# Folding the attention matrix into w_in: fp32 products, and three passes over two rounded parts

## The chip, the cores and the metric

The kernel runs on one core of a Trainium2 chip. The metric is the device time of one execution in microseconds. A core has TensorE (PE in the profile; its weight loads are PEld), VectorE (DVE), ScalarE (ACT), GpSimd (POOL) and the queue SP, from which all large transfers of this kernel are started.

## What is computed

The reference, cut to what matters (all operands are drawn at random; N = 6016 tokens, C = 256):

```python
qn = q / (norm(q, axis=1) + 1e-6);  kn = k / (norm(k, axis=1) + 1e-6)
a = softmax(kn.T @ qn / tau)             # 256 x 256
x = v @ a                                # 6016 x 256
h = x @ w_in                             # w_in 256 x 2048
x = maximum(0.01 * h, h) @ w_out         # w_out 2048 x 256
g = 1 / (1 + exp(-(x @ w_gate)))         # w_gate, w_val 256 x 1536
out = (g * (x @ w_val)) @ w_out2         # w_out2 1536 x 256
```

`w_in` and the other feed-forward weights come as 64-bit floats.

## The kernel before, in words

**Attention.** In the first 40 us the 6016 rows of q and k stream in, TensorE sums their products in fp32, and VectorE their squares. A short chain then makes `e`, the exponentials of the 256 x 256 scores, in two halves of 128 rows, and `zs`, the reciprocals of the row sums. TensorE turns each half (L398), and ScalarE copies it to `eT[i]` (L401).

**W'.** v @ a is never formed. Instead the kernel multiplies a into w_in once: W' = a @ w_in, 256 x 2048, in eight column groups j of 256. `w_half(j, i, o)` (L217) makes half i of W' of group j: two fp32 products (L221) of `eT[i]` with the columns of `win[j]`, 128x256 each; `w_prime` makes both halves side by side in PSUM bank b. The groups 0 and 1 are made in the preparation, in banks y0 to y3; the other six one by one in the loop over vT pair 0, group j + 2 in the turn of group j. `w_evac` (L258) takes W' out of PSUM on ScalarE, scaled by `zs`, and `split_blocks` (L241, L242) rounds it.

**Two rounded parts.** From W' on, all large products are made of two parts of each operand: `high` is a rounding to float32r on ScalarE, `low` the remainder, a subtraction on VectorE or GpSimd. Three matmuls (low x high, high x low, high x high) make one product; see `Core.mul` (L472), `Plain.block` (L523) and `Group.sum` (L573 to L576).

**Units.** A `Unit` is one 256 x 512 or 512 x 256 piece of a 64-bit weight. `act` (L170, L172) reads its two halves of each word on ScalarE; `join` (L176, L177, L183) puts them together as fp32 on VectorE, in a tile `s`. `win[j]` is the joined tile of unit `ins[j]`, and TensorE reads it as it is. A joined unit of w_out1 (`outs1`) is split into `wo` by a cast on VectorE (L206) and a subtraction on GpSimd (L207).

**Stages.** The tokens are worked through in six pairs of 512 + 512 (the last 448 + 448), first the two layers of the first network (kind 1), then the gated one (kind 2). In kind 1 a turn is one pair and one group j of 256 columns. In pair 0 a turn has four plain blocks (`Plain`: banks d, b, then a, c), six matmuls each; in later pairs and in kind 2 a seven-product scheme (`Core`).

**What sets the order.** The schedule is written by hand: each engine carries out its instructions in the order of the code. A turn j of pair 0 (L709 to L753) is, on TensorE: blocks d and b; the sums of the keys 22 and 12 of the turn before (L573 to L576); W' of group j + 2 in bank b; the sums of the keys 11 and 21; blocks a and c (in turn 0 there are no sums, and a and c come ahead of W'). ScalarE: `g22`, `g12` out of d and b (L554), their high parts `gh` (L548), the `act` of two units, `w_evac`, the split of W', then `g11`, `g21` and theirs. VectorE: the low parts `gl` of 22 and 12 (L549), the joins of two units and the cast of a `wo`, the low part of the split of W', `gl` of 11 and 21, and the low part of the block sums (L273). GpSimd: the subtraction of `wo` (L207) and the block sums (L264 to L267). The two units of turn j are `ins[j + 3]` and `outs1[j + 1]`. A bank is given on only when its reader is done: W' of group j + 2 needs `g12` read out of b, and block b of the next turn needs `w_evac`.

**End of the preparation** (L407 to L436). On VectorE: the join of `outs1[0]` (L424), the splits of W' of groups 0 and 1, the low parts of the tokens B11 and B21, the join of `ins[2]`. Pools: `s` has three buffers; the tile `w8` of 4 KB per partition (one buffer) is used only in later pairs.

Of the kernel before, what the change touches and what calls it, by code (L numbers as in the profile page):

```python
# [12 lines left out]
F32 = mybir.dt.float32  # L13
F32R = mybir.dt.float32r
I32 = mybir.dt.int32
U32 = mybir.dt.uint32
AF = mybir.ActivationFunctionType
ALU = mybir.AluOpType
# [4 lines left out]
P = 128  # L23
N = 6016
C = 256
F1 = 2048
F2 = 1536
KC = C // P
CH = 512
# [28 lines left out]
def attention_two_ffn(ctx, tc, q, k, vT, tau, w_in, w_out1, w_gate, w_val, w_out2, outT):  # L58
# [19 lines left out]
    nc = tc.nc  # L78

    def f32(ap):  # L80
        return ap.bitcast(F32)
# [7 lines left out]
    ps = ctx.enter_context(tc.tile_pool(name="ps", bufs=1, space=PSUM))  # L89
    cctx = ctx.enter_context(ExitStack())  # L90
    cv = cctx.enter_context(tc.tile_pool(name="cv", bufs=2, side=right))
    eT = [cv.tile([P, C], F32, name=f"eT{i}", bufs=1) for i in range(KC)]

    tau_sb = const.tile([P, 1], F32, name="tau_sb")
    zs = [const.tile([P, 1], F32, name=f"z{i}") for i in range(KC)]
# [50 lines left out]
    def cols(w, j):  # L146
        return w.bitcast(I32)[:, j * 512:(j + 1) * 512].rearrange("(a p) f -> p a f", p=P)

    def rows(w, j):
        return w.bitcast(I32)[j * 256:(j + 1) * 256, :].rearrange("(a p) f -> p a f", p=P)  # L150

    class Unit:
# [19 lines left out]
            nc.scalar.activation(self.c, lo.bitcast(U32), AF.Copy, scale=2.0**-29)  # L172

        def begin_join(self):
            s = self.s = cv.tile([P, CH], I32, tag="s", name="s", bufs=3)
            nc.vector.tensor_scalar(s, self.hi, -0x80000000, None, ALU.bitwise_and)  # L176
            nc.vector.scalar_tensor_tensor(  # L177
                s, self.x.bitcast(I32), 3, s, ALU.logical_shift_left, ALU.bitwise_or
            )
# [35 lines left out]
    win = {}  # L215

    def w_half(j, i, o):  # L217

        w = f32(win[j]).rearrange("p (a b) -> p a b", a=2)
        for jj in range(KC):  # L220
            nc.tensor.matmul(  # L221
                o, eT[i][:, jj * P:(jj + 1) * P], w[:, jj, :], start=jj == 0, stop=jj == KC - 1
            )
        return o

    def w_prime(j, wp):
        return [w_half(j, i, wp[:, i * 256:(i + 1) * 256]) for i in range(KC)]

    ins = [Unit(cols(w_in, j)) for j in range(G1)]
    outs1 = [Unit(rows(w_out1, j)) for j in range(G1)]  # L230
# [13 lines left out]
    def split_half(j, i, wp):  # L244

        src = wp.rearrange("p (a b) -> p a b", a=2)
        st, a = s1_t[j], a21_t[j]
        todo = [(st[:, :, 1:3], src)]
        if i == 0:
            todo = [(a[:, :, 0:1], src[:, 0:1]), (st[:, :, 0:1], src[:, 1:2])]  # L250
        for o, x in todo:
            nc.scalar.activation(o[:, 0], x, AF.Copy, scale=zs[i])
        for o, x in todo:
            nc.vector.scalar_tensor_tensor(o[:, 1], x, zs[i], f32(o[:, 0]), ALU.mult, ALU.subtract)
# [24 lines left out]
    with tc.manual_schedule():  # L279


        with ExitStack() as actx:
# [3 lines left out]
            sm = actx.enter_context(tc.tile_pool(name="sm", bufs=1))  # L286
# [36 lines left out]
            for gi, g in enumerate(GROUPS):  # L323
# [5 lines left out]
                for nm, src in (("k", kt), ("q", qt)):  # L329
                    a = accs[nm]  # L330
                    s2 = sq.tile([P, 4, C], F32, tag="s2" + nm, name="s2")
                    nc.scalar.activation(s2[:, :g, :], src[:, :g, :], AF.Square)
                    w = min(g, WIDTH[gi])
# [3 lines left out]
                    if gi + 1 < ng and WIDTH[gi + 1] < WIDTH[gi]:  # L337
                        w = WIDTH[gi + 1]
# [16 lines left out]
            for j, (nm, i) in enumerate((("k", 0), ("k", 1), ("q", 0), ("q", 1))):  # L355
                s = slice(i * P, (i + 1) * P)
# [18 lines left out]
            )  # L375
            rq = sm.tile([P, C], F32, name="rq")
            e_sb = []

            def scaled(i):
                s_sb = sm.tile([P, C], F32, tag=f"s_sb{i}", name="s_sb")  # L380
# [40 lines left out]
            turned(1)  # L421
            for w in (B12, B22):
                tok.low(w, nc.vector)
            o1_0 = outs1[0].join()  # L424
            split_half(0, 0, wp0[0][0])
            inverse(1)
            for j in range(2):
# [5 lines left out]
            split_half(1, 1, wp0[1][1])  # L433
            for w in (B11, B21):
                tok.low(w, nc.vector)
            win[2] = ins[2].join()  # L436


        s_b = ctx.enter_context(tc.tile_pool(name="s_b", bufs=5, reuse_waits="tile"))
# [5 lines left out]
        def o_tile(name):  # L445
            return op.tile([P, 2, 2, C], F32R, tag="o", name=name)
# [217 lines left out]
        for i, (kind, p, j) in enumerate(groups):  # L664
# [44 lines left out]
            if kind == 1 and p == 0:  # L709
# [21 lines left out]
                unsummed = unsummed[len(now):]  # L731
                for w, jj, u in units:
                    if w == "in":
                        win[jj] = u.join()
                    else:
                        o1_t[jj] = o_tile("wo")
                        split_rows(u.join(), o1_t[jj], nc.gpsimd)
# [142 lines left out]
```

## Time and profile before

| | us |
|---|---|
| median of 3 runs | 1094.44 (1094.23 to 1094.81) |
| the profiled execution | 1093.51 |
| its span, first to last instruction | 1091.4 |
| TensorE busy | 1081.2 (99%) |
| VectorE busy | 774.6 (71%) |
| ScalarE busy | 604.6 (55%) |
| GpSimd busy | 522.2 (48%) |
| DMA, share of 16 engines (the kernel's main queue) | 21.6% |

The profiled execution is one run of its own, 0.93 us below the median. The granted TensorE clock is 1.00 of full speed in every stretch of it. A busy share is an average over stages with different limits; the rows further down are taken from the stretch that the change touches. Start times are microseconds from the first instruction. Matmul records overlap: the time from one start to the next is what one costs in a row of them.

### The profile page before, as it was taken

Reading aid. Unit: us, or ns where it says so; the run is one execution under the profiler, and the core shown is the slowest. Engines: PE = TensorE matmul, PEld = TensorE weight load, DVE = VectorE, ACT = ScalarE, POOL = GpSimd, SP = SyncE. Lnnn points to the kernel's source line nnn. Section 1 sums busy time; section 2 is a strip of 40 time slices with the busy share of each in tenths; the row PEclk is TensorE's granted clock in tenths of the full one; section 3 lists DMA queues with packets and bytes.
Section 4 is the critical chain, followed back from the end, with each engine's and each line's share of the span. In section 5 each row is a group of like instructions: output and inputs, shape, how many; then the busy total and the mean of one; then the engine's idle time right before and its main releaser. Section 6 shows DMA issues by size and latency. Waiting matters only on the chain.

```text
span 1091.4 us, 13956 instructions
## 1 busy us (share of the span) xinstructions
PE 1081.2 (99%) x4842; PEld 907.2 (83%) x4842; DVE 774.6 (71%) x1059; ACT 604.6 (55%) x1055; POOL 522.2 (48%) x435
## 2 busy tenths in 40 slices
PE   9999999999999999999999999999999999999998
PEld 8878888888878888879988888888888888888997
DVE  7899945785776766773467777687677677667765
ACT  7787655676665675665553444454354345344433
POOL 0155327567657658656544424433534532443333
PEclk9999999999999999999999999999999999999999
DMA  9632221224241224238430001002002001000100
GB/s 351 256 113 81 78 77 53 92 58 145 89 153 49 78 73 145 73 112 322 155 135 1 1 20 59 1 0 77 1 1 77 1 1 47 27 1 1 39 1 35
DMA packets 31495, 84.01 MB, mean 77 GB/s; under 512 B 3008, under 2 KB 5824, under 8 KB 31424
## 3 DMA queue, kind: packets, MB, share of 16 engines
q1 hardware_dynamic: 31392, 83.11, 21.6%
q8 instruction: 38, 0.62, 0.2%
q14 instruction: 33, 0.27, 0.1%
q0 software_dynamic: 32, 0.00, 0.0%
HBM read 56.62 MB, written 26.48 MB: 76 GB/s over the span
## 4 chain that ended last, share of the span: by engine, by line
PE 92%; DVE 4%; DMA 2%; ACT 1%; issue 1%; SPq 0%; ACTq 0%; DVEq 0%
PE c L472 13%; PE y L576 13%; PE d L472 13%; PE y L573 13%; PE y L574 13%; PE a L472 13%; PE b L472 7%; DMA kt<-in_k 2%; PE wp L221 1%; PE a L523 1%; PE c L523 1%; PE b L523 1%; PE d L523 1%; DVE accq L336 1%; PE s L315 1%
## 5 line engine op out<-in xcount | busy, mean ns | idle before, releaser
L573 PE MATMUL y<-gh,wo 128*128 128x512 f32 (+1 forms) x672 | 259.8, 387 | 0.0
L574 PE MATMUL y<-gh,wo 128*128 128x512 f32 (+1 forms) x672 | 258.8, 385 | 0.0
L549 POOL TENSOR_TENSOR gl<-v,gh 128x512 fp32r<-128x512 f32 (+1 forms) x76 | 107.2, 1410 | 292.1 <-issue 187.1
L576 PE MATMUL y<-gl,wo 128*128 128x512 f32 (+1 forms) x672 | 205.2, 387 | 0.0
L472 PE MATMUL c<-tok,s 128*128 128x512 f32 (+1 forms) x672 | 186.3, 385 | 3.0 <-DVE c L501 2.9
L472 PE MATMUL d<-tok,s 128*128 128x512 f32 (+1 forms) x672 | 186.2, 385 | 0.0
L472 PE MATMUL a<-tok,s 128*128 128x512 f32 (+1 forms) x672 | 185.9, 385 | 0.0
L501 DVE TENSOR_TENSOR c<-u,c 128x512 f32<-128x512 f32 (+1 forms) x112 | 75.6, 675 | 138.9 <-PE c L472 133.5
L472 PEld LDWEIGHTS c<-tok,s 128*128 128x128 f32 x672 | 125.8, 188 | 27.6 <-DVE c L501 4.2
L576 PEld LDWEIGHTS y<-gl,wo 128*128 128x128 f32 x672 | 125.4, 188 | 25.9 <-POOL gl L549 2.8
L472 PEld LDWEIGHTS d<-tok,s 128*128 128x128 f32 x672 | 125.9, 188 | 24.0 <-DVE u L506 0.8
L573 PEld LDWEIGHTS y<-gh,wo 128*128 128x128 f32 x672 | 126.2, 188 | 23.5
L574 PEld LDWEIGHTS y<-gh,wo 128*128 128x128 f32 x672 | 126.2, 188 | 23.4
L472 PEld LDWEIGHTS a<-tok,s 128*128 128x128 f32 x672 | 126.2, 188 | 23.4
L549 POOL TENSOR_TENSOR gl<-c,gh 128x512 fp32r<-128x512 f32 (+1 forms) x76 | 99.9, 1314 | 83.3 <-ACT gh L548 50.0
L486 DVE TENSOR_TENSOR u<-u,a 128x512 f32<-128x512 f32 (+1 forms) x112 | 75.2, 671 | 38.8 <-PE a L472 35.7
L549 POOL TENSOR_TENSOR gl<-u,gh 128x512 fp32r<-128x512 f32 (+1 forms) x75 | 97.5, 1300 | 0.0
L472 PE MATMUL b<-tok,s 128*128 128x512 f32 (+1 forms) x336 | 92.9, 385 | 0.0
L483 ACT COPY u<-b 128x512 f32<-128x512 f32 (+1 forms) x112 | 64.8, 579 | 48.2 <-PE b L472 48.0
L548 ACT CAST gh<-v 128x512 fp32r<-128x512 f32 (+1 forms) x76 | 46.5, 612 | 78.3 <-DVE v L832 75.5
L489 DVE TENSOR_TENSOR v<-u,c 128x512 f32<-128x512 f32 (+1 forms) x112 | 75.7, 676 | 13.6 <-DVE u L486 0.5
L491 DVE TENSOR_TENSOR v<-v,d 128x512 f32<-128x512 f32 (+1 forms) x112 | 75.7, 676 | 11.7
(125 smaller groups left out, 1522.1 us busy)
## 6 DMA issues: line engine op xcount, KB each, us to landing
wr<-in_moe_w_out SPq DMA_DIRECT2D x14, 512.0 KB, 4.1
g_d<-st SPq DMA_DIRECT2D x6, 896.0 KB, 3.6
v_d<-st SPq DMA_DIRECT2D x6, 896.0 KB, 3.6
s<-g_d SPq DMA_DIRECT2D x6, 896.0 KB, 5.6
s<-v_d SPq DMA_DIRECT2D x6, 896.0 KB, 6.3
x_d<-o SPq DMA_DIRECT2D x20, 256.0 KB, 3.2
outT<-o SPq DMA_DIRECT2D x20, 256.0 KB, 2.0
kt<-in_k SPq DMA_DIRECT2D x9, 512.0 KB, 9.8
```

What stands on the lines that cost most here:

```text
L472: nc.tensor.matmul(o[:, :n], self.st[:, w, kind, :], t[:, x, :n], start=first and i == 0, stop=i == 2, skip_group_check=not first,)
L483: nc.scalar.copy(u[:, :n], self.b[:, :n])
L486: nc.vector.tensor_tensor(u[:, :n], u[:, :n], self.a[:, :n], ALU.add)
L489: nc.vector.tensor_tensor(v[:, :n], u[:, :n], self.c[:, :n], ALU.add)
L491: nc.vector.tensor_tensor(v[:, :n], v[:, :n], self.d[:, :n], ALU.add)
L501: nc.vector.tensor_tensor(t[:, :n], self.u[:, :n], self.c[:, :n], ALU.add)
L523: nc.tensor.matmul(o[:, :self.n], w, x, start=i == 0, stop=i == len(todo) - 1)
L548: nc.scalar.copy(gh[:, :n], src[:, :n])
L549: eng.tensor_tensor(gl[:, :n], src[:, :n], f32(gh[:, :n]), ALU.subtract)
L573: nc.tensor.matmul(acc[c, m][:, :n], wo[:, 1, e, s[m]], gh, start=first, stop=False)
L574: nc.tensor.matmul(acc[c, m][:, :n], wo[:, 0, e, s[m]], gh, start=False, stop=False)
L576: nc.tensor.matmul(acc[c, m][:, :n], wo[:, 0, e, s[m]], gl, start=False, stop=stop)
```

## The change

The six products of W' from group 2 on are made of rounded parts, like the others. `eT[i]` gets a split copy `eTr[i]` (high on ScalarE, low on VectorE) at the end of the preparation. Each `win[j]`, j from 2, goes through `split_win`: the high part is a cast on ScalarE, the low part a subtraction on GpSimd, into the one buffer of tag `w8`. `w_half` then issues six float32r matmuls in three passes where it issued two fp32 ones. `eT` moves to the pool `sm`, which closes with the attention part; `s` has two buffers instead of three. The join of `outs1[0]` moves from ahead of the splits of W' to behind the join of `ins[2]`.

```diff
--- before.py
+++ after.py
@@ -89,7 +89,8 @@
     ps = ctx.enter_context(tc.tile_pool(name="ps", bufs=1, space=PSUM))
     cctx = ctx.enter_context(ExitStack())
     cv = cctx.enter_context(tc.tile_pool(name="cv", bufs=2, side=right))
-    eT = [cv.tile([P, C], F32, name=f"eT{i}", bufs=1) for i in range(KC)]
+    eT = []
+    eTr = [cv.tile([P, 2, C], F32R, name=f"eTr{i}", bufs=1) for i in range(KC)]
 
     tau_sb = const.tile([P, 1], F32, name="tau_sb")
     zs = [const.tile([P, 1], F32, name=f"z{i}") for i in range(KC)]
@@ -172,7 +173,7 @@
             nc.scalar.activation(self.c, lo.bitcast(U32), AF.Copy, scale=2.0**-29)
 
         def begin_join(self):
-            s = self.s = cv.tile([P, CH], I32, tag="s", name="s", bufs=3)
+            s = self.s = cv.tile([P, CH], I32, tag="s", name="s")
             nc.vector.tensor_scalar(s, self.hi, -0x80000000, None, ALU.bitwise_and)
             nc.vector.scalar_tensor_tensor(
                 s, self.x.bitcast(I32), 3, s, ALU.logical_shift_left, ALU.bitwise_or
@@ -216,11 +217,22 @@
 
     def w_half(j, i, o):
 
-        w = f32(win[j]).rearrange("p (a b) -> p a b", a=2)
-        for jj in range(KC):
-            nc.tensor.matmul(
-                o, eT[i][:, jj * P:(jj + 1) * P], w[:, jj, :], start=jj == 0, stop=jj == KC - 1
-            )
+        if j < 2:
+            todo = [(eT[i], f32(win[j]))]
+        else:
+            todo = [(eTr[i][:, x], win[j][:, w]) for x, w in ((1, 0), (0, 1), (0, 0))]
+        todo = [
+            (a[:, jj * P:(jj + 1) * P], b[:, jj * 256:(jj + 1) * 256])
+            for a, b in todo for jj in range(KC)
+        ]
+        for t, (a, b) in enumerate(todo):
+            nc.tensor.matmul(o, a, b, start=t == 0, stop=t == len(todo) - 1)
+        return o
+
+    def split_win(s):
+        o = cv.tile([P, 2, CH], F32R, tag="w8", name="win", bufs=1)
+        nc.scalar.copy(o[:, 0], f32(s))
+        nc.gpsimd.tensor_tensor(o[:, 1], f32(s), f32(o[:, 0]), ALU.subtract)
         return o
 
     def w_prime(j, wp):
@@ -375,6 +387,7 @@
             )
             rq = sm.tile([P, C], F32, name="rq")
             e_sb = []
+            eT += [sm.tile([P, C], F32, name=f"eT{i}") for i in range(KC)]
 
             def scaled(i):
                 s_sb = sm.tile([P, C], F32, tag=f"s_sb{i}", name="s_sb")
@@ -421,7 +434,6 @@
             turned(1)
             for w in (B12, B22):
                 tok.low(w, nc.vector)
-            o1_0 = outs1[0].join()
             split_half(0, 0, wp0[0][0])
             inverse(1)
             for j in range(2):
@@ -433,7 +445,11 @@
             split_half(1, 1, wp0[1][1])
             for w in (B11, B21):
                 tok.low(w, nc.vector)
-            win[2] = ins[2].join()
+            for a, b in zip(eT, eTr):
+                nc.scalar.copy(b[:, 0], a)
+                nc.vector.tensor_tensor(b[:, 1], a, f32(b[:, 0]), ALU.subtract)
+            win[2] = split_win(ins[2].join())
+            o1_0 = outs1[0].join()
 
 
         s_b = ctx.enter_context(tc.tile_pool(name="s_b", bufs=5, reuse_waits="tile"))
@@ -731,7 +747,7 @@
                 unsummed = unsummed[len(now):]
                 for w, jj, u in units:
                     if w == "in":
-                        win[jj] = u.join()
+                        win[jj] = split_win(u.join())
                     else:
                         o1_t[jj] = o_tile("wo")
                         split_rows(u.join(), o1_t[jj], nc.gpsimd)
```

What stands where on VectorE at the end of the preparation and at the start of turn 0, before (`wr_384` is `outs1[0]`, `wr_386` is `ins[2]`, `wr_559` and `wr_568` are `ins[3]`, `s_485` is the joined `outs1[0]`; its join stands 11 rows further up, ahead of the splits of W'):

```order
L143 TENSOR_TENSOR tok_503<-raw_380,tok_503 128x512
L143 TENSOR_TENSOR tok_505<-raw_380,tok_505 128x512
L176 TENSOR_SCALAR s_515<-wr_386 128x512
L177 SCALAR_TENSOR_TENSOR s_515<-x_475,s_515 128x512
L183 ISA s_515<-s_515,c_477 128x1024
L206 CAST wo_538<-s_485 128x512
L549 TENSOR_TENSOR gl_601<-g22_596,gh_600 128x512
L549 TENSOR_TENSOR gl_605<-g12_598,gh_604 128x512
L176 TENSOR_SCALAR s_631<-wr_559 128x512
```

and with the change:

```order
L450 TENSOR_TENSOR eTr0_75<-eT0_424,eTr0_75 128x256
L450 TENSOR_TENSOR eTr1_76<-eT1_425,eTr1_76 128x256
L177 TENSOR_SCALAR s_517<-wr_386 128x512
L178 SCALAR_TENSOR_TENSOR s_517<-x_477,s_517 128x512
L184 ISA s_517<-s_517,c_479 128x1024
L177 TENSOR_SCALAR s_524<-wr_384 128x512
L178 SCALAR_TENSOR_TENSOR s_524<-x_440,s_524 128x512
L184 ISA s_524<-s_524,c_442 128x1024
L207 CAST wo_547<-s_524 128x512
L565 TENSOR_TENSOR gl_618<-g22_613,gh_617 128x512
L565 TENSOR_TENSOR gl_622<-g12_615,gh_621 128x512
L177 TENSOR_SCALAR s_648<-wr_568 128x512
```

Two subtractions for eTr and the join of `outs1[0]` now stand between the tokens' low parts and `gl` of turn 0, and the join of `ins[3]` is behind them.

ScalarE at the same place, before (`d_563` and `b_570` are the blocks of turn 0, `x_608` belongs to `ins[3]`):

```order
L252 ACTIVATE s_467<-wp_498,z1_79 128x256 [waits PE_49]
L554 ACTIVATE g22_596<-d_563 128x512 [waits PE_49,Activation_49]
L554 ACTIVATE g12_598<-b_570 128x512 [waits PE_49,Activation_49]
L548 CAST gh_600<-g22_596 128x512 [waits Activation_49]
L548 CAST gh_604<-g12_598 128x512 [waits Activation_49]
L170 ACTIVATE x_608<-wr_559 128x512 [waits DMAHW7_49]
```

and with the change:

```order
L264 ACTIVATE s_469<-wp_496,z1_79 128x256 [waits PE_49]
L449 CAST eTr0_75<-eT0_424 128x256 [waits Activation_49]
L449 CAST eTr1_76<-eT1_425 128x256 [waits Activation_49]
L234 CAST win_521<-s_517 128x512 [waits DVE_49]
L570 ACTIVATE g22_613<-d_572 128x512 [waits DVE_49,PE_49]
L570 ACTIVATE g12_615<-b_579 128x512 [waits PE_49]
L564 CAST gh_617<-g22_613 128x512 [waits Activation_49]
L564 CAST gh_621<-g12_615 128x512 [waits Activation_49]
L171 ACTIVATE x_625<-wr_568 128x512 [waits DMAHW7_49]
```

`g22` and `g12` of turn 0 stand behind the cast of win[2], which waits for VectorE's join of `ins[2]`.

ScalarE further on in turn 0, before (`wp_591` and `wp_600` are W' of group 2 in bank b):

```order
L258 ACTIVATE wt_620<-wp_459,z0_78 128x256
L258 ACTIVATE wt_620<-wp_495,z1_79 128x256
L258 ACTIVATE wt_623<-wp_460,z0_78 128x256
L258 ACTIVATE wt_623<-wp_498,z1_79 128x256
L258 ACTIVATE wt_642<-wp_591,z0_78 128x256 [waits PE_49]
L258 ACTIVATE wt_642<-wp_591,z1_79 128x256
L241 CAST a21_646<-wt_642 128x128 [waits Activation_49]
L241 CAST s_645<-wt_642 128x384 [waits Activation_49]
L554 ACTIVATE g11_651<-a_577 128x512
```

and with the change:

```order
L270 ACTIVATE wt_637<-wp_461,z0_78 128x256
L270 ACTIVATE wt_637<-wp_493,z1_79 128x256
L270 ACTIVATE wt_640<-wp_462,z0_78 128x256
L270 ACTIVATE wt_640<-wp_496,z1_79 128x256
L234 CAST win_652<-s_648 128x512 [waits DVE_49,PE_49,Pool_49]
L270 ACTIVATE wt_662<-wp_600,z0_78 128x256
L270 ACTIVATE wt_662<-wp_600,z1_79 128x256
L253 CAST a21_666<-wt_662 128x128 [waits Activation_49]
L253 CAST s_665<-wt_662 128x384 [waits Activation_49]
L570 ACTIVATE g11_671<-a_586 128x512
```

The cast of win[3], with waits for VectorE, TensorE and GpSimd, stands ahead of the two instructions that empty bank b. The later turns have the same form.

## Rows read from the trace of the kernel before

**Rows 1.** Busy line of the page: busy us (share of the span) xinstructions, by engine.

```profile
PE 1081.2 (99%) x4842; PEld 907.2 (83%) x4842; DVE 774.6 (71%) x1059; ACT 604.6 (55%) x1055; POOL 522.2 (48%) x435
```

**Rows 2.** Table by stretch, vT pair 0: busy us (instructions) of each engine.

```profile
core 0: us, PE busy (x) PEld busy (x) DVE busy (x) ACT busy (x) POOL busy (x), PEclk, DMA share, GB/s
...
67.40:80.20 12.80, 12.77 (x57) 10.64 (x57) 12.28 (x16) 9.83 (x21) 9.59 (x12) 1.00 0.40 134
```

**Rows 3.** Waits of 57 to 133 us: who waited for whom, us, times, longest.

```profile
ACT a L241 <- PE c L523: 16.5, 5, 4.0
...
PEld wp L221 <- ACT g L554: 0.5, 1, 0.5
PEld b L523 <- ACT wt L258: 0.4, 1, 0.4
```

**Rows 4.** Chain that ended last, 0 to 180 us: start, us, what.

```profile
59.97 1.73 PE wp L221 x8
...
63.07 1.66 PE b L523 x6
...
67.48 1.99 PE wp L221 x8
```

**Rows 5.** The same chain, three matmuls of 512 and of 448 columns.

```profile
148.56 0.68 PE c L472 x3
...
1041.33 0.61 PE d L472 x3
```

**Rows 6.** Timeline of VectorE, 56 to 65 us: start, us, line, out<-in, xcount.

```profile
56.44 1.28 DVE L143 TENSOR_TENSOR tok<-raw,tok 128x512 fp32r<-128x512 f32 x2
57.64 0.42 DVE L176 TENSOR_SCALAR s<-wr 128x512 int32<-128x512 int32 x1
...
59.44 0.42 DVE L206 CAST wo<-s 128x512 fp32r<-128x512 f32 x1
59.78 2.36 DVE L549 TENSOR_TENSOR gl<-g,gh 128x512 fp32r<-128x512 f32 x2
62.06 0.69 DVE L176 TENSOR_SCALAR s<-wr 128x512 int32<-128x512 int32 x1
...
64.41 0.68 DVE L176 TENSOR_SCALAR s<-wr 128x512 int32<-128x512 int32 x1
```

**Rows 7.** Timeline of ScalarE, 53 to 68 us: also [idle before <-releaser].

```profile
53.46 0.48 ACT L252 ACTIVATE s<-wp,z 128x256 fp32r<-128x256 f32 x1 [1.01 <-DVE z L405]
...
60.75 2.27 ACT L258 ACTIVATE wt<-wp,z 128x256 f32<-128x256 f32 x6
62.89 0.32 ACT L241 CAST a<-wt 128x128 fp32r<-128x128 f32 x1
...
66.84 0.59 ACT L554 ACTIVATE g<-b 128x512 f32<-128x512 f32 x1
67.32 1.13 ACT L548 CAST gh<-g 128x512 fp32r<-128x512 f32 x2
```

**Rows 8.** Timeline of GpSimd, its subtraction of 128x512, twice.

```profile
59.99 1.60 POOL L207 TENSOR_TENSOR wo<-s,wo 128x512 fp32r<-128x512 f32 x1 [19.86 <-DVE wo L206]
...
123.38 1.40 POOL L207 TENSOR_TENSOR wo<-s,wo 128x512 fp32r<-128x512 f32 x1 [4.86 <-DVE wo L206]
```

**Rows 9.** Timeline of VectorE, 120 to 132 us, and one row of TensorE.

```profile
120.80 0.42 DVE L176 TENSOR_SCALAR s<-wr 128x512 int32<-128x512 int32 x1
...
122.88 0.43 DVE L206 CAST wo<-s 128x512 fp32r<-128x512 f32 x1
123.22 0.42 DVE L176 TENSOR_SCALAR s<-wr 128x512 int32<-128x512 int32 x1
...
126.20 0.43 DVE L206 CAST wo<-s 128x512 fp32r<-128x512 f32 x1
...
130.07 1.82 DVE L549 TENSOR_TENSOR gl<-g,gh 128x512 fp32r<-128x512 f32 x2
...
131.62 0.62 PE L576 MATMUL y<-gl,wo 128*128 128x512 f32 x2
```

## The prediction

> **What bounds the kernel now.** I read first the page's busy line: TensorE is busy 1081.2 of 1091.4 us [rows 1]. So a microsecond of TensorE work taken out, or of waiting put in, moves the end by a microsecond unless it sits in the first 57 us, where TensorE still waits for data. All the products that change lie between 59 and 120 us, so I read that stretch next. The table by stretch shows that there VectorE is as full as TensorE: 12.28 of 12.80 us [rows 2]. The list of waits of 57 to 133 us says whether that busy time hides slack: none of its six rows is VectorE's, so it runs one instruction after the other for all that time; TensorE waits for ScalarE twice, 0.5 and 0.4 us; ScalarE alone has room, 16.5 us in five waits for TensorE [rows 3]. So three engines run a tight relay in vT pair 0: TensorE fills bank b, ScalarE empties it, VectorE makes the low parts that TensorE needs one turn later. The chain shows the handovers: W' of group 2 at 59.97, then block b of the next turn at 63.07, W' of group 3 at 67.48 [rows 4]. Both later ones use bank b, and both waited for ScalarE [rows 3].
>
> **TensorE's part.** One of six products today is 8 records in 1.73 us, 0.216 each (each fp32 product is two passes) [rows 4]. The change issues 12 one-pass matmuls of 256 columns. No row has that form. Three float32r matmuls of 512 columns take 0.68, of 448 columns 0.61 [rows 5]: 0.227 and 0.203 each, so 64 columns are worth 0.024 and 256 columns come to 0.13. That is 1.56 per product, 0.17 less, 1.0 us over six. Lower bound 0.11, half of the 512-column row; upper bound 0.216, what one fp32 pass over 256 columns takes today. I take 0.13, because both float32r rows are of the very instruction, with other weights before each, and only the column count differs.
>
> **The preparation.** The join of the first w_out1 unit leaves its place ahead of the first split of W'. ScalarE waited 1.01 us for VectorE's reciprocal there [rows 7]; what then limits is the W' product itself, so the rest comes some 0.25 us earlier (an estimate; it lies between 0 and 0.3). The last `low` on VectorE then ends at 57.4 instead of 57.64 [rows 6].
>
> From there I follow one chain, in the order of the listing ahead of this:
>
> - Two eT subtractions, 128x256. The nearest row is 1.28 for two of 128x512 [rows 6], so 0.3 each, with overhead up to 0.42; 0.35 gives 58.1.
> - Join of ins[2]: 57.64 to 59.44, 1.80 [rows 6]: 59.9.
> - ScalarE's new cast of 128x512 waits for it: 0.6, as the gh casts (1.13 for two) [rows 7]: 60.5. Behind it on ScalarE stand g22 and g12 of turn 0, which used to start at once. They take 0.49 and 0.59 [rows 7], so bank b, which W' of group 2 needs, is free at 61.6, not before 59.97. GpSimd's remainder (1.40 and 1.60 on the nearest rows, for the same shape [rows 8]) ends near 62; W' of group 2 ends near 63.5 instead of 61.70.
> - VectorE: the moved w_out1 join, 1.80 alone. GpSimd's new subtraction falls on it. What that costs is shown by two joins of one turn (5): 120.80 to 122.88, 2.08, with GpSimd idle (4.86 us ahead of 123.38 [rows 8]); 123.22 to 126.20, 2.98, under GpSimd's subtraction of 1.40 [rows 8, 9]. So 0.9 more: 62.6. Then the cast, 0.34: 62.95; gl22 and gl12 as before, 2.28: 65.2; join of ins[3] as before, 2.35: 67.6, where it ends at 64.41 before [rows 6]. VectorE is now 3.2 late.
> - ScalarE's cast for win[3] waits for that join: 68.2. The evacuation of W' of group 2 stands *behind* it: two instructions, 0.38 each (2.27 for six [rows 7]): 69.0. Block b of turn 1 needs the bank: 69.0 instead of 63.07. **TensorE is 5.9 us late.**
> - W' of group 3 waits for g12 of turn 1, which follows that evacuation by 4.5 us (62.89 to 66.84 plus 0.59 [rows 7]): 73.5 instead of 67.48, 6.0 late. The five products that are left give back 5 x 0.17: **5.1 late** by this chain.
>
> **A second chain, VectorE.** It has no wait until after 133 us, so nothing absorbs what is added: 3.2 late after turn 0, and five more subtractions on GpSimd, each issued while VectorE joins the w_out1 unit, at 0.9: 7.7 late. The low part of key 11 of turn 5 was ready at about 131.0 (130.07 and half of 1.82 [rows 9]), and TensorE's use of it starts at 131.62 [rows 9]: 0.6 of slack. So this chain puts TensorE 7.1 late. The two chains overlap and do not add; the later one counts. After 133 us VectorE has its waits back, TensorE is dense to the end, and what was lost stays lost.
>
> **Hidden, costed at nothing:** the eT casts on ScalarE (they end before the VectorE work that they feed), the five later casts of win on ScalarE themselves (0.6 each, beside its 16.5 us of waits [rows 3]; without that cover 3 us), the pair of `s` buffers in place of three (the readers on GpSimd are done a join earlier), the later loads of the units (they are issued later with the joins, and need not land until some 4 us after).
>
> **Sum.** +7.1 us. On the profiled execution, 1093.51, that is 1100.6; the median of the runs shown is 0.93 above it, 1094.44 + 7.1 = **1101.5 us**. Bounds: if a GpSimd subtraction costs VectorE nothing, the second chain has 2.3 - 0.6 = 1.7 and the first decides, with 5.0 at block b and 4.2 at the end: 1098.6. If it costs its whole 1.40, 2.3 + 6 x 1.40 - 0.6 = 10.1: 1104.5. With 0.216 a matmul the first chain decides, as rival 3 works out: 1104.7.
>
> The row says that 0.9 of GpSimd's 1.40 us are lost. [...]
>
> **Rivals.**
>
> 1. *The cover holds; not slower.* TensorE's gain of 1.0 and the 0.25 of the preparation come through: 1093.2, within 0.2%. The point that decides is ScalarE's cast ahead of the evacuation: the join of ins[3] must end by 61.7, so that 0.6 and 0.75 more still meet 63.07. For it: the work is only moved or given to engines with idle time. Against it: I get 67.6, and even before the change that join ended at 64.41 [rows 6]. Chance 0.05.
> 2. *VectorE's fullness is elastic.* Its instructions stretch beside GpSimd, and re-timed they might run at their short durations (gl pair 1.28, join 2.08). Then only the moved and the waiting work stays: joins to 59.9 and 61.7, cast 62.05, gl 63.3, join 65.4, ScalarE's cast and evacuation 66.8: 3.7 late, 3.8 at W' of group 3, 3.0 at the end: 1097.4. Against it: GpSimd gets more work there, not less. Chance 0.09.
> 3. *The passes are not cheaper.* If a float32r matmul of 256 columns took what one fp32 pass takes, 0.216, a product would be 2.59, 0.86 more: 6.0 + 5 x 0.86 = 10.3, 1104.7. This is also the case of the change not doing what it says. Against it: float32r at 512 columns is one record of 0.227 [rows 5]. Chance 0.06.
> 4. *Whole exclusion*: each GpSimd subtraction stops VectorE for all of its 1.40 us: 1104.5, as above. For it: VectorE's pair took 2.36 under one of 1.60 and 1.28 without [rows 6, 8], so 1.08 were lost; against it: the join's 0.9. Chance 0.08. [...]
>
> **How the numbers follow.** The forecast, both chains at work, has 0.72. The range from 1097.0 to 1104.7 takes in the bounds of lock and matmul, and leaves out rival 1, half of rival 2 and what lies above 3 and 4. A measurement of this kernel tells about 0.2%, 2.2 us, from no change: up to 1096.6 is "same". Forecast, rivals 3 and 4 and most of rival 2 are slower: 0.90; rival 1 and the rest of 2 are the same: 0.08; faster would need more than TensorE has to gain: 0.02.
>
> **What would show it.** In the changed profile: ScalarE's first win cast starting near 59.9 and g22 only behind it; a TensorE gap of several us ahead of block b of turn 1, ended by ScalarE's `wt`; W' as 12 records at about 0.13; joins of the w_out1 units near 3.0 instead of 2.0; VectorE still without a wait near 130 and later than before by more than TensorE's 0.6 of slack. I am wrong if block b of turn 1 starts within 2 us of 63.07, if TensorE shows no wait longer than 1 us after 60 us, or if VectorE's lateness does not grow from turn to turn.

## The result and the profile after

| | before | after |
|---|---|---|
| median, same chip (6 runs each) | 1094.38 us (1093.54 to 1094.81) | 1102.11 us (1100.86 to 1103.87) |
| ratio after / before, 95% interval | | 1.0072 [1.0062, 1.0082] |
| profiled execution; its span | 1093.51; 1091.4 | 1100.86; 1098.9 |

The change makes the kernel slower by 7.7 us, 0.7%. Forecast were 1101.5 us, 7.1 more than before, in a range of 1097.0 to 1104.7. Of the six runs of the changed kernel, three lie at 1100.9 to 1101.3 with a mean granted clock of 0.997 and three at 1102.9 to 1103.9 with 0.995; the profile is one of the first three.

The page of the changed kernel: the busy line (as [rows 1]), and the chain that ended last, by engine.

```profile
PE 1083.6 (99%) x4866; PEld 908.5 (83%) x4866; DVE 780.6 (71%) x1061; ACT 608.3 (55%) x1063; POOL 530.1 (48%) x441
...
PE 85%; DVE 9%; DMA 2%; ACT 2%; issue 2%; SPq 0%; DVEq 0%; ACTq 0%
```

The chain of the kernel before:

```profile
PE 92%; DVE 4%; DMA 2%; ACT 1%; issue 1%; SPq 0%; ACTq 0%; DVEq 0%
```

TensorE is "99% busy" before and after; that line shows nothing. The chain does: VectorE's share of it was 4% before and is 9% now. Followed in order of time, the path that sets the end runs on VectorE from 56 to 118 us, over ScalarE's casts and evacuations to 130, and on VectorE again to 138.6.

The list of waits of 57 to 150 us, the longer ones of TensorE and ScalarE (who waited for whom, us in total, times, longest):

```profile
ACT win L234 <- DVE s L184: 17.7, 6, 4.3
...
PE b L539 <- ACT wt L270: 3.0, 2, 2.6
...
PE wp L229 <- ACT g L570: 1.9, 1, 1.9
```

TensorE waited 0.5 us at most in this stretch [rows 3]. Now it has two gaps, of 1.9 and 2.6 us, and both are the relay over bank b (a third wait for the bank, 0.4, comes at 120). The same list for VectorE is empty from 57 to 143 us.

TensorE's timeline, the rows that answer to [rows 4]:

```profile
61.63 3.06 PE L229 MATMUL wp<-win,eTr 128*128 128x256 f32 x12 [1.87 <-ACT g L570]
64.49 1.31 PE L539 MATMUL d<-tok,a 128*128 128x512 f32 x3
...
69.10 2.93 PE L539 MATMUL b<-tok,s 128*128 128x512 f32 x6 [2.62 <-ACT wt L270]
71.83 0.60 PE L589 MATMUL y<-gh,wo 128*128 128x512 f32 x1
...
140.57 1.53 PE L539 MATMUL a<-tok,s 128*128 128x512 f32 x6
```

The last of them is block a of turn 6, the first block behind all products of W'. In the kernel before it stood here:

```profile
133.44 1.52 PE L523 MATMUL a<-tok,s 128*128 128x512 f32 x6
```

Block b of turn 1 starts 6.0 later than at 63.07. And it takes 2.93 in place of 1.66, W' of group 2 3.06. Why, the table by stretch shows (busy us of each engine, then PEclk, the granted clock):

```profile
59.90:61.60 1.70, 0.00 (x0) 0.00 (x0) 1.63 (x4) 1.62 (x4) 0.93 (x1) 1.00 0.00 0
61.60:64.50 2.90, 2.81 (x13) 2.60 (x14) 2.87 (x4) 2.90 (x6) 1.75 (x2) 0.57 0.00 0
...
66.50:69.10 2.60, 0.00 (x0) 0.00 (x0) 2.30 (x4) 1.41 (x4) 2.52 (x4) 0.95 0.70 201
69.10:71.90 2.80, 2.80 (x7) 2.23 (x8) 2.69 (x4) 2.74 (x7) 1.71 (x2) 0.50 0.63 188
```

TensorE does nothing in the first and the third row, and behind each gap its granted clock falls, to 0.57 in the second row and to 0.50 in the fourth; before, it was 1.00 throughout.

VectorE's timeline at the same place, and GpSimd's:

```profile
52.26 0.35 DVE L266 SCALAR_TENSOR_TENSOR a<-wp,z,a 128x128 fp32r<-128x128 f32 x1 [1.69 <-ACT s L264]
...
57.40 0.75 DVE L450 TENSOR_TENSOR eTr<-eT,eTr 128x256 fp32r<-128x256 f32 x2
58.07 0.42 DVE L177 TENSOR_SCALAR s<-wr 128x512 int32<-128x512 int32 x1
...
61.04 1.65 DVE L184 CUSTOM_DVE_ANT_0 s<-s,c 128x1024 uint16<-128x1024 uint16 x1
62.72 0.43 DVE L207 CAST wo<-s 128x512 fp32r<-128x512 f32 x1
63.06 2.38 DVE L565 TENSOR_TENSOR gl<-g,gh 128x512 fp32r<-128x512 f32 x2
65.37 0.41 DVE L177 TENSOR_SCALAR s<-wr 128x512 int32<-128x512 int32 x1
...
69.18 1.55 DVE L184 CUSTOM_DVE_ANT_0 s<-s,c 128x1024 uint16<-128x1024 uint16 x1
...
137.59 1.81 DVE L565 TENSOR_TENSOR gl<-g,gh 128x512 fp32r<-128x512 f32 x2
```

```profile
60.67 1.47 POOL L235 TENSOR_TENSOR win<-s,win 128x512 fp32r<-128x512 f32 x1 [20.76 <-ACT win L234]
63.28 1.61 POOL L208 TENSOR_TENSOR wo<-s,wo 128x512 fp32r<-128x512 f32 x1 [1.15 <-DVE wo L207]
...
68.45 1.72 POOL L235 TENSOR_TENSOR win<-s,win 128x512 fp32r<-128x512 f32 x1
```

The last step of a w_out1 join (L184) takes 0.69 alone and 1.55 to 1.65 under GpSimd's new subtraction, in all six turns. Lay the three pairs of rows side by side: GpSimd ends at 62.14, 64.89 and 70.17, and the VectorE instruction that was issued meanwhile at 62.69, 65.44 and 70.73, each time 0.55 behind it. At the end of pair 0 VectorE makes the first low part of key 11 of turn 5 at 137.59 in place of 130.07 [rows 9]: 7.52 late.

ScalarE's timeline, the two casts and what stands behind them:

```profile
59.98 0.62 ACT L234 CAST win<-s 128x512 fp32r<-128x512 f32 x1 [3.76 <-DVE s L184]
60.50 0.59 ACT L570 ACTIVATE g<-d 128x512 f32<-128x512 f32 x1
60.99 0.59 ACT L570 ACTIVATE g<-b 128x512 f32<-128x512 f32 x1
...
67.69 0.62 ACT L234 CAST win<-s 128x512 fp32r<-128x512 f32 x1 [1.33 <-DVE s L184]
68.22 0.83 ACT L270 ACTIVATE wt<-wp,z 128x256 f32<-128x256 f32 x2
```

ScalarE stood idle for 3.8 us with g22 and g12 behind the cast, and later for 1.3 with the evacuation of bank b behind the next.

From there TensorE's lateness goes: W' of group 3 at 74.79 (7.3 late), of group 5 at 99.47 (6.6), of group 6 at 111.81 (6.3), block a of turn 6 at 140.57 in place of 133.44 (7.1). Between groups 4 and 6 it regains 0.28 a turn. At turn 5 it loses 0.5 at block b, which waits for an evacuation behind a win cast, which waits for VectorE's join; 0.3 at W' of group 7; and 0.4 at key 11, where it waits for VectorE's first low part. After turn 6 the instructions of both kernels run at the same distance, but for one wait of 0.3 at 487 us, to the end: 7.5.

### The profile page after: what moved, and what is told of

It is laid out like the page before. It is cut to its first block, busy times and chain, and to the rows that moved or that the text cites. A ratio compares the mean times of both kernels' runs of the same rounds, so it can differ in the third digit from the quotient of the medians.

```text
span 1098.9 us, 14010 instructions
## 1 busy us (share of the span) xinstructions
PE 1083.6 (99%) x4866; PEld 908.5 (83%) x4866; DVE 780.6 (71%) x1061; ACT 608.3 (55%) x1063; POOL 530.1 (48%) x441
## 4 chain that ended last, share of the span: by engine, by line
PE 85%; DVE 9%; DMA 2%; ACT 2%; issue 2%; SPq 0%; DVEq 0%; ACTq 0%
PE d L488 13%; PE c L488 13%; PE a L488 13%; PE y L592 12%; PE y L589 12%; PE y L590 12%; PE b L488 7%; DMA qt<-in_q 2%; DVE gl L565 2%; DVE s L184 1%; DVE s L178 1%; DVE s L177 1%; DVE tok L144 1%; DVE s L254 1%; PE s L327 1%
```

## The experiments

All kernels are edits of the changed one. "Late" is against the profile of before. Profiles differ by up to 0.6 us in when the preparation ends (the low parts of the last tokens start at 56.20 in the profile of after, 56.15 to 56.83 in the others), and why is not shown; so a few tenths of any single start mean nothing.

| kernel | median us | ratio to before | block b of turn 1: start, its record | key 11 of turn 5, VectorE | block a of turn 6 |
|---|---|---|---|---|---|
| before | | | 63.07, 1.66 | 130.07 | 133.44 |
| after | 1102.11 | 1.0072 | 69.10, 2.93 | 137.59 | 140.57 |
| cast late | 1102.69 | 1.0078 [1.0063, 1.0093] | 67.03, 2.92 | 138.46 | 141.39 |
| remainder on VectorE | 1100.65 | 1.0061 [1.0044, 1.0077] | 68.88, 1.66 | 136.27 | 139.22 |
| no remainder | 1098.98 | 1.0043 [1.0028, 1.0058] | 68.81, 1.67 | 133.44 | 137.73 |
| no moved join | 1101.18 | 1.0062 [1.0047, 1.0077] | 68.27, 2.93 | 137.14 | 140.11 |
| gaps filled | 1101.66 | 1.0065 [1.0049, 1.0080] | 69.55, 1.66 | 138.08 | 141.03 |

The median of before was 1093.6 beside the four in the middle, 1094.75 beside the last.

### The win cast behind the evacuation

```diff
-                        win[jj] = split_win(u.join())
+                        held = (jj, u.join())
...
                     w_evac(wt, wp)
+                    if held is not None:
+                        win[held[0]] = split_win(held[1])
```

> In the turns of vT pair 0 the cast of win (and with it GpSimd's subtraction) stands behind the evacuation of W' on ScalarE instead of ahead of it. Two chains: block b of turn 1 starts near 67.2 instead of 69.10 and no longer at half clock, and yet the end hardly moves, since VectorE is as late as before (first gl of key 11 of turn 5 at 137.6, within 0.5) and TensorE must wait for it there, now longer: block a of turn 6 at 140.6 again, 1101.5 to 1102.5 us. Relay alone (only the cast ahead of the evacuation costs): 1.9 from the bank and 1.4 from the clock come back, 1098.8 us.

The relay was relieved as meant: block b of turn 1 came 2.1 sooner, W' of group 5 at 97.75 (4.9 late in place of 6.6). The end did not follow: TensorE stood still again, for ScalarE's g12, for GpSimd's remainder and longest for VectorE's low part, in TensorE's timeline:

```profile
123.84 0.50 PE L229 MATMUL wp<-win,eTr 128*128 128x256 f32 x2 [0.71 <-ACT g L570]
124.64 1.45 PE L229 MATMUL wp<-win,eTr 128*128 128x256 f32 x10 [0.29 <-POOL win L235]
...
139.45 0.73 PE L592 MATMUL y<-gl,wo 128*128 128x512 f32 x2 [1.55 <-DVE gl L565]
```

So the relay alone does not set the time; VectorE's chain does. Two things came otherwise than expected: block b's record was as long as at the clock of 0.50 in the changed kernel (2.92, and 2.93 there), and VectorE was 0.87 later than after, where at most 0.5 was allowed. Why it lost more is not worked out here.

### The remainder of win on VectorE

```diff
-        nc.gpsimd.tensor_tensor(o[:, 1], f32(s), f32(o[:, 0]), ALU.subtract)
+    def low_win(o, s):
+        nc.vector.tensor_tensor(o[:, 1], f32(s), f32(o[:, 0]), ALU.subtract)
```

(called behind the join of the turn's w_out1 unit)

> The remainder of win is subtracted on VectorE, behind the join of the w_out1 unit, instead of on GpSimd. Two chains with 0.87 lost for each GpSimd subtraction: VectorE now pays 0.61 itself, so the first gl of key 11 of turn 5 comes 6 x 0.26 = 1.6 earlier, near 136.0, and the time is 1100.5 us. If GpSimd's subtraction stood in nobody's way, VectorE would be 3.7 later, gl at 141.3 and 1105.8 us. If it stopped VectorE for its whole 1.47, gl comes 5.2 earlier, near 132.4, and the bank-b chain decides, near 1100 us.

Doing the subtraction on VectorE itself, 0.68 each, is cheaper for VectorE than having GpSimd do it: 1.3 sooner at key 11 of turn 5, 1.7 if the later start of this profile (56.60) is taken off. Both are as expected. GpSimd's help costs VectorE more here than the work it takes over: 0.86 to 0.96 in the rows of L184 above, against 0.68. The rows show it; the time, 7.0 over its before in place of 7.7, does not by itself, since the intervals of the two ratios overlap.

### The remainder left out

The remainder of win is not computed, and its pass reads the high part in its place.

```diff
-        nc.gpsimd.tensor_tensor(o[:, 1], f32(s), f32(o[:, 0]), ALU.subtract)
...
-            todo = [(eTr[i][:, x], win[j][:, w]) for x, w in ((1, 0), (0, 1), (0, 0))]
+            todo = [(eTr[i][:, x], win[j][:, 0]) for x, w in ((1, 0), (0, 1), (0, 0))]
```

> The remainder of win is not computed; the pass that used it reads the high part once more, so TensorE does as much as with the change. Two chains: VectorE gets 6 x 0.87 = 5.2 back, first gl of key 11 of turn 5 near 132.4; what is left is the bank-b chain: block b of turn 1 near 68.2, still at half clock, 0.3 a turn regained, 1099.3 us. If GpSimd costs VectorE nothing, gl stays at 137.6 and the time at 1102.1 us. If the subtraction costs its whole 1.47, gl near 129, and the time again 1099 us.

VectorE is 3.4 late at key 11 of turn 5, 4.1 less than after, and it waits again, where in the changed kernel it had no wait (the list of waits of 57 to 133 us):

```profile
DVE a L253 <- ACT a L252: 0.8, 2, 0.6
```

Now the relay is what decides: block b of turn 1 is still 5.7 late, W' of group 5 is 5.1 late, and 0.28 a turn comes back until block a of turn 6, 4.3 late. From block b of turn 5 to block a of turn 6 TensorE takes 6.80 us, as in the kernel before; in the changed kernel it took 7.20. Otherwise than expected, block b took no longer than at the clock of 1.00 before (1.67, and 1.66 there). The page of this kernel:

```profile
PE 91%; DVE 4%; DMA 2%; ACT 1%; issue 1%; SPq 0%; ACTq 0%; DVEq 0%
```

VectorE's share of the chain is 4% again; but that share says little, since it is 4% as well with the remainder on VectorE and without the moved join. Six subtractions on GpSimd put VectorE back by 4.1 to 4.8 (0.6 is the difference of the starts), and with the 0.8 that it now waits they cost it 4.9 to 5.6, 0.8 to 0.9 each. They cost the end less, 2.3 (7.7 over before, against 5.4), since the first chain then decides.

### The first w_out1 join left out

The first w_out1 unit is not joined; its split reads the joined win[2].

```diff
-            win[2] = split_win(ins[2].join())
-            o1_0 = outs1[0].join()
+            o1_0 = ins[2].join()
+            win[2] = split_win(o1_0)
```

> The join of the first w_out1 unit is left out (its split reads the joined win[2] instead), so that nothing has moved into VectorE's way there. It took 1.80 alone and 2.65 under GpSimd's subtraction. Order decides: gl of key 22 of turn 0 cannot start ahead of its gh, which stands behind the cast of win[2] on ScalarE and ends at 62.1, so VectorE gets only 1.0 to 1.2 of the 2.65 back: block b of turn 1 near 68.0, first gl of key 11 of turn 5 near 136.5, 1101.0 us. If the moved join were the cause with its full 2.65: gl near 135.0, block b near 66.4, 1099.5 us.

1.8 us of VectorE's work is gone, and 0.5 to 0.9 of it arrives at key 11 of turn 5, as expected. VectorE waits 1.7 for `gh` in turn 0, since ScalarE's casts still stand where they stood:

```profile
60.42 0.43 DVE L207 CAST wo<-s 128x512 fp32r<-128x512 f32 x1
62.57 2.22 DVE L565 TENSOR_TENSOR gl<-g,gh 128x512 fp32r<-128x512 f32 x2 [1.72 <-ACT gh L564]
```

### The gaps of TensorE filled

```diff
+                    fill(0, 14, g.tok)
                 wp = w_prime(j + 2, bank("b", "wp")) if j + 2 < G1 else None
...
+                if self.st is s1_t[1]:
+                    fill(1, 20, self.tok)
```

> The changed kernel with filler matmuls on TensorE, whose results nothing reads: 14 of 256 columns ahead of W' of group 2 and 20 ahead of block b of turn 1, each into half of a bank that is in no other use then, so that TensorE is busy in its two gaps. Theory (two chains; VectorE's decides the end, the half clock of block b of turn 1 lies beside it): block b of turn 1 still starts at 69.1, but takes 1.36 in place of 2.73, since the clock stays at 1.00; W' of groups 3 to 6 start 1.3 sooner than in the changed kernel (73.5, 85.8, 98.1, 110.4), yet the first low part of key 11 of turn 5 is still made at 137.6 and block a of turn 6 still starts at 140.3 to 140.6: median 1101.5 to 1102.2. Rival (the half clock decides): block a of turn 6 starts at 139.2 or sooner, median 1100.7 or less. Second rival (the clock falls for another reason than the gaps): block b of turn 1 still takes 2.7.

The table by stretch of this kernel, over the two former gaps and block b:

```profile
59.90:61.60 1.70, 1.70 (x15) 1.66 (x14) 1.63 (x4) 1.14 (x3) 0.44 (x1) 1.00 0.00 0
66.50:69.10 2.60, 2.60 (x20) 2.44 (x20) 2.36 (x4) 1.26 (x4) 2.52 (x5) 1.00 0.52 160
69.10:71.90 2.80, 2.39 (x11) 1.96 (x11) 2.63 (x5) 2.74 (x8) 1.71 (x2) 1.00 0.68 223
```

With TensorE busy in the gaps the clock stays at 1.00 and block b takes 1.66. So in the changed kernel, with 0.50 on block b, it is the gaps that bring the clock down. W' of group 3 comes at 73.96 in place of 74.79, although this profile starts 0.5 later. Yet the time is that of the changed kernel, and block a of turn 6 is no sooner: the 1.3 us lie beside VectorE's chain.

### The splitting laid out anew

Five kernels in a row, to see whether the loss is in the work or in where it stands. Each is an edit of the one ahead of it.

```diff
-        nc.gpsimd.tensor_tensor(o[:, 1], f32(s), f32(o[:, 0]), ALU.subtract)
+        nc.vector.tensor_tensor(o[:, 1], f32(s), f32(o[:, 0]), ALU.subtract)
...
+    def split_out(s, o):
+        w = f32(s).rearrange("p (a b) -> p a b", a=2)
+        nc.scalar.copy(o[:, 0], w)
+        nc.vector.tensor_tensor(o[:, 1], w, f32(o[:, 0]), ALU.subtract)
...
-            todo = [(eTr[i][:, x], win[j][:, w]) for x, w in ((1, 0), (0, 1), (0, 0))]
+            todo = [(eTr[i][:, x], win[j][:, w]) for x, w in ((1, 0), (0, 0), (0, 1))]
```

> The same products in three passes, but the splitting laid out anew: eT is split while VectorE still waits for W' of groups 0 and 1; win of group 2 is cast behind g22 and g12; every later win is cast behind the evacuation; the remainders of win and of w_out1 are taken on VectorE, none on GpSimd, and w_out1 is cast on ScalarE; the last step of the first w_out1 join stands behind the first low parts; the pass that needs the remainder of win comes last. Theory (the passes are cheaper, and all the time that was lost is in where the splits stand and in VectorE working beside GpSimd): no wait of TensorE over 0.6 us after 60, W' as 12 records in about 1.4, six products 0.3 each under before, 1.8 in all: median 1092.2 to 1093.4, 1 to 2 us faster than before. Rival (the splitting is too much work for VectorE's time in these turns, wherever it stands): 0.7 for each of 6 remainders of win is added to VectorE, less its 0.6 of slack, block a of turn 6 3 to 4 us late: median 1096 to 1098. Second rival (ScalarE, with 6 more casts of win and 6 of w_out1, now evacuates too late): waits of block b on wt in several turns, median 1094 to 1096.

1100.51 us (1099.77 to 1103.04), ratio 1.0058 [1.0045, 1.0071]: a miss. Neither rival's place was the one either. The profiled run is the longest, 1103.04. Most is lost at one wait, which TensorE's timeline shows (another, 1.6 for the win cast, stands ahead of W' of group 2):

```profile
66.16 1.90 PE L546 MATMUL b<-tok,s 128*128 128x512 f32 x6
...
74.46 2.93 PE L229 MATMUL wp<-win,eTr 128*128 128x256 f32 x12 [3.66 <-ACT g L577]
```

Block b of turn 1 is only 3.1 late now. But g12 of turn 1, which frees bank b for W' of group 3, stands on ScalarE behind the casts and scalings of turn 0, and behind that gap the clock is 0.50, from 74.4 to 80.0. From turn 2 on TensorE waits for nothing, and VectorE waits again. ScalarE's timeline shows a cause that the prediction had not seen:

```profile
60.13 0.60 ACT L577 ACTIVATE g<-d 128x512 f32<-128x512 f32 x1 [4.09 <-DVE s L177]
```

No cast of win is ahead of g22 here, and still it starts at 60.13. It waits for the first step of the w_out1 join: with that join moved back, the unit's raw words are read later. They lie in a pool that closes with the attention part, and the wait says that g22's tile takes their memory; the addresses are not shown. In the next kernel, where the join stands early again, g22 starts at 56.56 and has no such wait. The changed kernel has the same wait, hidden behind the cast: the first step of that join ends at 60.28 there, the cast at 60.60.

```diff
+            o1_0 = outs1[0].join()
             for w in (B11, B21):
                 tok.high(w)
...
+                if j == 1:
+                    behind()
```

(`behind` holds the keys 11 and 21 of the turn before, its `wo` and its block sums; it is called behind g22 and g12.)

> The kernel of the run before (all remainders on VectorE), with ScalarE's order of turns 0 and 1 laid out anew: the first w_out1 unit is joined as early as its `s` buffer allows, ahead of the second half of W' of group 1, and cast as soon as it is there; g22 and g12 of turn 0 follow at once; the two units of turn 0 are scaled around the first win cast; W' of group 2 is evacuated ahead of W' of group 1; g22 and g12 of turn 1 stand ahead of keys 11 and 21 of turn 0. Theory (what was lost in the run before was lost only in ScalarE's order at W' of group 3, where TensorE waited 3.7 us for g12): W' of group 3 starts at 67 to 69 in place of 74.5, no wait of TensorE over 0.7 after 60, and later W' regain 0.3 a turn: median 1093 to 1095, no more than 0.1% from before on either side. Rival (ScalarE and VectorE together have no room in turns 0 and 1, in any order): another wait of 2 us or more shows up between 60 and 80, median 1096.5 or more.

1094.86 us (1094.18 to 1095.81, 11 runs) against 1094.41, ratio 1.0004 [0.9995, 1.0013], as expected, though with one wait more than that: W' of group 3 starts at 67.85 (74.46 in the run ahead), that of group 4 waits 1.5 for g12.

```diff
-                if j == 1:
+                if j in (1, 2):
                     behind()
...
-                if j:
+                if j > 1:
                     behind()
```

> The kernel of the run before with one more step of the same kind: g22 and g12 of turn 2 too stand ahead of keys 11 and 21 of the turn before. Theory (TensorE's 1.5 us of waiting at W' of group 4 came from that place in ScalarE's order and from nothing else): W' of group 4 starts at 80.2 to 80.6 in place of 81.9, TensorE waits no longer than 0.8 anywhere between 57 and 145, block a of turn 6 starts at 132.4 to 132.9 (before: 133.44), median 1093.2 to 1094.0, 0 to 0.1% under before. Rival (VectorE or GpSimd set that moment anyway): W' of group 4 or of group 5 waits 1 us or more again, median as in the run before, 1094.5 to 1095.2.

1096.48 us (1094.86 to 1098.44; the profiled run took 1097.70), ratio 1.0020 [1.0011, 1.0029]. W' of group 4 came at 80.43, as the theory had it, and the rival's wait came as well, a turn later and longer:

```profile
80.43 1.60 PE L229 MATMUL wp<-win,eTr 128*128 128x256 f32 x12
...
95.38 2.74 PE L229 MATMUL wp<-win,eTr 128*128 128x256 f32 x12 [2.44 <-ACT g L589]
```

Ahead of it, in the timelines of VectorE and GpSimd, a VectorE pair takes 3.51 us (1.28 alone) under a GpSimd sum of 2.66 for the next token pair:

```profile
83.31 3.51 DVE L577 TENSOR_TENSOR gl<-g,gh 128x512 fp32r<-128x512 f32 x2
```

```profile
83.01 2.66 POOL L126 TENSOR_TENSOR sums<-raw 128x1024 f32<-128x1024 f32 x1 [6.12 <-DMA raw<-in_vT]
```

That pair alone is not the source. A VectorE pair takes 3.51 at this place in the run ahead as well (82.38) and in the last one (82.51), and neither has such a wait. Here g12 of turn 3 also stands on ScalarE behind the keys 11 and 21 and the `wo` of turn 2, and these wait for the late VectorE.

```diff
-            o1_0 = outs1[0].join()
+            outs1[0].begin_join()
...
             in_2 = ins[2].join()
+            o1_0 = outs1[0].end_join()
```

> The same, and the last step of the first w_out1 join stands behind the join of the unit for win of group 2, with its cast on ScalarE behind that of win. Theory (the 0.7 and 0.3 us that TensorE waited ahead of W' of group 2 are that join's place on VectorE): W' of group 2 starts at 59.9 to 60.2 in place of 60.6, block b of turn 1 at 62.9 to 63.3 in place of 63.77, block a of turn 6 at 131.8 to 132.4: median 1092.5 to 1093.4, 0.1 to 0.2% under before. Rival (ScalarE's order there is tight as well: the later cast and scalings push W' of group 3): W' of group 3 waits 1 us or more, median 1094 or more.

1096.86 us, ratio 1.0022 [1.0013, 1.0031]. W' of group 2 came as expected, at 60.05; block b of turn 1 did not, at 63.64, since W' waited 0.4 for VectorE's remainder in its midst. The same wait of 2.4 at W' of group 5 took back more than was gained.

```diff
-                if j in (1, 2):
+                if 0 < j < 6:
                     behind()
...
-                if j > 1:
+                if j > 4:
                     behind()
```

> The kernel of the run before with the order of ScalarE that freed bank b in time at W' of groups 3 and 4 kept in every turn: g22 and g12 of a turn ahead of keys 11 and 21 of the turn before, up to turn 5. Theory (W' of group 5 waited 2.4 us only because that order ended with turn 2, after GpSimd's sum of 2.7 us had held VectorE up): W' of group 5 starts at 92.5 to 93.2 in place of 95.2, none of TensorE's waits between 57 and 145 is over 0.8, its clock stays at 1.00, block a of turn 6 starts at 132.0 to 132.8 (before: 133.44): median 1092.8 to 1094.0, 0 to 0.15% under before. Rival (VectorE, which that sum of GpSimd's delays by 2.2 us, is the bound again from turn 2 on): W' of group 6 or 7, or the low parts of turn 5, come 1 us or more late, median 1095 or more.

1093.57 us (1093.16 to 1094.19, 11 runs) against 1093.66, ratio 0.9998 [0.9989, 1.0008]. No wait of TensorE is over 0.42 in the stretch, and the table by stretch has it busy 86.84 of 88 us (this kernel first, then the kernel before the change):

```profile
57.00:145.00 88.00, 86.84 (x413) 72.09 (x412) 74.02 (x113) 71.05 (x140) 29.55 (x35) 1.00 0.27 84
```

```profile
57.00:145.00 88.00, 87.86 (x388) 72.49 (x387) 78.59 (x106) 63.19 (x126) 42.66 (x43) 1.00 0.27 84
```

Block a of turn 6 starts at 133.60, where 132.0 to 132.8 were expected: two waits of 0.4 for VectorE's remainders are left, and the start of W' of group 2 is 0.7 later than before. With that, what the cheaper passes give, 0.28 a product, is used up. All of the loss was in places and in GpSimd's overlap, which these kernels change together; laid out well, the change is worth nothing that can be measured either way. The new order could not have helped the kernel before: there TensorE stands still for only 0.14 of the 88 us. A version that beats both kernels was not found.

## Why the prediction was right, point by point

- **TensorE's part.** W' of group 3 runs from 74.79 to 76.22, 12 matmuls in 1.43, 0.119 each where 0.13 was taken; a turn gives back 0.28, not 0.17. Rival 3 (0.216) is out.
- **The preparation** came 0.24 sooner (56.20 for 56.44), 0.25 was taken; that is luck. VectorE made the reciprocals of the first half at 47.38 in place of 47.60, so 0.22 was there ahead of the join's old place. Where the join had stood, VectorE now waits 1.69 for ScalarE (the first row of its timeline above), and ScalarE waits 1.00 for the next reciprocal, as before (1.01). Moving the join gave nothing there.
- **The first chain** stood nearly to the tenth, up to block b of turn 1 (forecast, then measured end): join of ins[2] 59.9, 59.94; cast 60.5, 60.60; bank b free 61.6, 61.58; join of the w_out1 unit 62.6, 62.69; both `gl` 65.2, 65.44; join of ins[3] 67.6, 67.58; evacuation 69.0, 69.05; block b starts 69.0, 69.10. The steps between are right; the start, and with it the last tenths, is the luck of the point above.
- **What it had half.** "Behind it on ScalarE stand g22 and g12" is right, and the time came out right, but g22 had a second reason to be late, its tile's memory (the first kernel laid out anew); taking the cast out of its way alone would have gained 0.2 there (from 60.50 to 60.28). The listing ahead of the prediction has the added wait of g22 for VectorE, and the working did not follow it up.
- **What it missed: the clock.** The step "W' of group 3 ... 73.5 ... 6.0 late" takes block b at full clock and lets W' wait for g12. Block b ran at 0.50 (2.93 for 1.66), and W' of group 3 came at 74.79; g12 was out at 73.45, and TensorE was at work from 69.10 on without a wait. The first chain is 7.3 late there and 6.3 at W' of group 6; two more products at 0.28 would have left it 5.8 late at its end (an estimate), not 5.1. It stayed the shorter of the two, so the sum did not move; had VectorE lost less, it would have been 0.7 us wrong.
- **The second chain** decided. Forecast: 3.2 late after turn 0 and 7.7 at key 11 of turn 5, less 0.6 of slack. Measured: 3.1 and 7.52, 0.88 more each turn, and block a of turn 6 7.13 late. Over the 5.8 of the first chain that is 1.3, so the two lie close together. The price of a subtraction on GpSimd, 0.9 by the row of a join, shows as 0.86 to 0.96 in the rows of L184 (1.55 to 1.65 for 0.69), and as 0.8 to 0.9 by leaving all six out.
- **GpSimd's price.** In the three pairs of rows above, what VectorE issued under GpSimd's instruction ended 0.55 behind it each time, so there VectorE was held up to its end. But the price is not GpSimd's whole 1.47, as rival 4 had it: the VectorE step ahead ran from 60.31 for 0.69 and was not held up by what GpSimd began at 60.67. In the two rows of L184 it goes with what was left of GpSimd's instruction when VectorE issued its own: 1.10 and 0.99 were left, and 0.96 and 0.86 were lost.
- **Rivals 1 and 2.** The cover did not hold (block b was 6 late, the point was 61.7 for a join that ended at 67.5), and VectorE was not elastic: the pair of `gl` took 2.38, not 1.28. In the chances, 0.90 for slower leaves 0.04 to rival 2, which is less than the "most" of its 0.09.
- **The median** is 0.6 above the forecast: 0.35 of that is the wait at 487 us. Where the rest comes from stays open: runs of this kernel spread over 3 us, of which one was profiled. In the profiles with the remainder on VectorE, without the remainder and without the moved join the matmuls of 448 columns take 368 ns in place of 365 between 1030 and 1085 us, far behind the stretch; in the last two of them the starts lie 0.206 to 0.207 us apart there in place of 0.2025, which over 60 us is 1.2 (an estimate).

## What to carry to other kernels

Work moved to engines with idle time on average need not be free: here the relay between the engines had no slack in that very stretch, and 1.7 us of cheaper products brought 7 us of lateness, while TensorE's busy share stayed at 99%. On an engine that frees a bank, put that instruction ahead of new work that waits for somebody else, and keep the order in every turn; here that paid only together with the rest of the new layout, since the evacuation ahead of the cast gained nothing by itself. Help from GpSimd was dear for a VectorE without waits: a subtraction of 0.68 on VectorE itself cost less than the same one on GpSimd beside it, 0.8 to 0.9.

## What was not expected of the hardware

- Behind gaps of 1.9 and 2.6 us TensorE's clock was granted at 0.57 and 0.50, and block b of turn 1 took 1.27 longer. Matmuls whose results nobody reads, put into the gaps, kept it at 1.00. The kernels differ: in those without the remainder and with it on VectorE, block b of turn 1 came nearly as late (68.81 and 68.88) and took 1.67 and 1.66. One wait of 1.5 us, in the second kernel laid out anew, left the clock at 1.00 (the mean from 80 to 145); behind one of 2.4, in the third, it was 0.60 from 95 to 98.
- GpSimd's sum of 2.66 us held a VectorE pair up for 2.2 (3.51 for 1.28), and again its end and VectorE's fit: 85.67 plus the 0.55 of the rows above plus 0.60 for the second of the pair is 86.82.
